# Attention front of a routed-expert kernel: values through four 32-row tiles, scores through two 64-row tiles

## The chip, the cores and the metric

The kernel runs on one core of one Trainium2 chip. The metric is the device time of one launch in microseconds, taken as the median of several runs. The engines named below are TensorE (PE for its matrix multiplications, PEld for its weight loads), VectorE (DVE), ScalarE (ACT), GpSimd (POOL) and SyncE (SP, which here only issues transfers).

## The reference

Two stages are computed. The first is an attention through 32 memory slots per head: for each of 8 batches and 8 heads, `phi` (576 tokens by 32 slots) is put through a softmax over the slots, keys and values are summed into the slots with these weights, and every query attends to the 32 slots. The second is a mixture of eight experts with exactly 576 tokens each: a greedy assignment by descending gate logit, then two matrix multiplications with a ReLU between them.

```python
a = exp(phi - max(phi)); a = a / (sum(a) + 1e-9)            # [8, 8, 576, 32]
k_m = einsum('bhsm,bhsd->bhmd', a, k); v_m = einsum('bhsm,bhsd->bhmd', a, v)
scores = (q @ k_m.T) / 8
attn = softmax(scores)                                       # over 32 slots
x = (attn @ v_m) as [4608 tokens, 512]
logits = x @ w_gate                                          # [4608, 8]
assigned = greedy by logit, 576 tokens to each expert
out[expert e] = relu(x[e] @ w1[e]) @ w2[e]                   # 512 -> 1024 -> 512
```

## The kernel before

**Front.** Function `front` computes the attention. The work of a batch is done once for each of the 8 batches: phi is loaded (`load_a`), its maximum is taken (`m1`, `mt`, `m2`, `bt`) and subtracted (`bs`, `sb`, on VectorE for the batches in `BD`, on GpSimd for the others), then the exponential (`ex`), the sums over tokens into the slots (`kv_`, 80 matrix passes in four column tiles, after `load_kv` has brought keys and values), the normalisers (`zm`, `zn`, `zs`), and the transposed keys (`kt`, `kb`) and values (`vc`, `vd`). `vg` and `vl` multiply the slot values by the gate weights and put the result in eight more columns beside the values, so that the router's logits come out of the same multiplication as the attention's output.

The queries come in 18 units of 256 tokens. Sixteen are half a batch each. Units 8 and 17 are the rests of four batches each; they use 32 tokens of each batch at a time, and are called rest units below. A unit goes through `SC` (scores; PSUM tile `sc`), `T1` (VectorE transposes 32 by 32), `MX` (maximum), `SB` (subtraction, GpSimd), `SE` (exponential, ScalarE), `SU` (sum and reciprocal, three VectorE instructions), `NM` (multiplication, GpSimd), `T2` (transposed back), `AV` (values, PSUM tile `av` out of three banks), `XC` (copy to `xs` on ScalarE), `ST` (store to the DRAM buffer `xd`). The head pairs of keys and values are kept as zero-padded operands: `kbd` holds each head's 64 rows of keys with 64 rows of zeros, and `vb` holds four heads' values as blocks of a 128 by 256 matrix whose other blocks are zeros, cleared once at the start (L1063).

For 13 units the logits come out of `AV`, in columns 256 to 263 of each of its four outputs, and VectorE copies or adds them into `lg` (`LO`, L1021 and L1024). For the five units in `DF` an own multiplication `LG` gives the logits early (`LC` copies them, L1017), and `AV` may come later.

All of these operations are ordered by a planner (`build`, `Sched`): it is given each operation's engine, a duration, what it needs, and a key, and writes one fixed program order for each engine. The engines then run their own lists in order and wait for each other by semaphores. The table `PRMS` holds the keys.

**Router.** From the logits, `r1` (four groups of token columns) finds each token's best margin, `sg` to `tT` find a threshold for every expert, `assign` picks the experts, `p1`, `p4a` and the `ll` multiplications make lists of token rows (`idx`). With the first five columns of `idx`, GpSimd gathers token rows from `xd` (L415).

**Experts.** `FFN.run` then works off eight experts. Each expert's weights are loaded, split in two parts of lower precision, and three multiplications are added for each product. This stage isn't touched.

The lines of the kernel that the prediction uses: L907 and L910 are `kv_`, L914 and L915 `zm`, L970 `SC`, L1006 `AV`, L1014 `LG`, L853 the load of keys and values, L856 that of a unit's queries, L1038 and L1043 the stores.

Of the kernel before, what the change touches and what calls it, by code (L numbers as in the profile page):

```python
# [67 lines left out]
class Router:  # L68
# [6 lines left out]
    def __init__(s,tc,lg,cf,fo,cb,bo,keep,out=None,ident=None):  # L75
# [9 lines left out]
        s.kp=keep; s.pq={}; s.lists={}; s.keep_il={}  # L85
    def begin(s,wk,ps,small,T,pos,il):

        s.wk=wk; s.ps=ps; s.small=lambda sh: ps.tile(sh,F32,name=small,bufs=2)
        s.tg=(pos,il)
        s.T=ps.tile([128,E],F32,name=T[0],bufs=T[1])  # L90
# [90 lines left out]
    def p1(s):  # L181
        nc=s.nc
        s.pos=s.ps.tile([128,289],F32,name=s.tg[0][0],bufs=s.tg[0][1])
# [39 lines left out]
    def RT(s,a,i):  # L223
        R,Rt,*x=s.lists[a]
        s.nc.vector.tensor_tensor(Rt[:,i],R,x[i],op=ALU.mult)
        if i and s.keep_il.get(a) is None:
            s.lists[a][4]=s.ps.tile([128,2,R.shape[2]],F32,name=s.tg[1][0],bufs=s.tg[1][1])
            if a: s.keep_il[a]=s.lists[a][4]
        if i: s.lists[a][4]=s.keep_il.get(a,s.lists[a][4])
# [386 lines left out]
class Sched:  # L616
# [67 lines left out]
    P=8.03, TQ=-25.59, CQ=-371.99, SC=-17.05, T1=-43.99, MX=38.12, SB=167.02, SE=6.14, T2=-53.03,  # L684
    AV=172.87, AVS=0.46, SU=-19.2, NM=22.34, XC=-91.14, LO=-48.45, ST=-63.73, EV=15, NP=3, NB=7, NQ=9,
    NK=2,
    UB=[4.67, 3.41, -1.23, -0.5, -5.71, -9.21, -5.08, 5.12, 2.83, -10.67, -26.24, 4.6, -0.08, 22.96, 4.55, 2.18, 2.71, 0.03],
    CF=163.65, CB=176.37, NA=3, BD=[0, 1, 2, 7], DF=[12, 13, 14, 15, 16], LG=56.71, LC=208.16,
    DA=305.18, DX=292.62, DS=238.38, R0=159.09, RK=-963.03, W1=257.31, WH=177.42, WS=304.44, WE=0,
    RV=[26, 10], la=-39.88, lk=-23.18, lq=3.93, lr=-16.74, m1=132.78, mt=-2.4, m2=-95.66, bt=3.2,  # L690
    bs=32.51, sb=5.74, ex=-99.2, ad=71.74, kv=-50.81, kvs=-2.43, zm=-31.99, zn=28.86, zs=88.73,
    vc=17.65, kt=30.28, vd=-43.5, kb=-149.94, vg=-8.21, vl=18.54,
    PB=[16.49, -24.8, 8.73, 2.34, -0.04, 30.67, -11.48, 4.98], slack=0, wend=30,
)
def build(X,f,B=8):
# [9 lines left out]
    for n in range(N):  # L705
        T=anch[n]+X['UB'][n]; b,bb,_=units[n]; rem=len(bb)>1
        op('SP',(1.35,3.3),T+X['SC']+X['lq'],lambda n=n:f.load_q(n),[],[('lq',n)],[('Q',X['NQ'],('Q',n))])
        for h in range(2):
            op('PE',1.1 if rem else .6,T+X['SC']+.5*h,lambda n=n,h=h:f.SC(n,h),[('lq',n)]+[('kb',x) for x in bb]+([('sc',n,0)] if h else []),[('sc',n,h)],[] if h else [('sc',1,('sc',n))],[('Q',n),('sc',n)]+[('KB',x) for x in bb])
# [9 lines left out]
        if df:  # L719
            op('PE',.9,T+X['LG'],lambda n=n:f.LG(n),[('t2',n)]+[('vl',x) for x in bb],[('lgm',n)],[('tp',2,('lgm',n))],[('pT',n)]+[('VB',x) for x in bb])  # L720
            op('DVE',.16,T+X['LC'],lambda n=n:f.LC(n),[('lgm',n)],[('lg',n)],[],[('lgm',n)])
        ta,tx,ts=(X['DA']+n,X['DX']+n,X['DS']+n) if df else (T+X['AV'],T+X['XC'],T+X['ST'])
        for j in range(4):
            op('PE',.56 if rem else .45,ta+X['AVS']*j,lambda n=n,j=j:f.AV(n,j),[('t2',n)]+[(i,x) for x in bb for i in ('vc','vl')],[('av',n,j)],[('av',X['NA'],('av',n,j))],[('pT',n)]+[('VB',x) for x in bb])
            if not df: op('DVE',.15,T+X['LO']+X['AVS']*j,lambda n=n,j=j:f.LO(n,j),[('av',n,j)]+([('lo',n,j-1)] if j%2 else []),[('lo',n,j)],[],[('av',n,j)])
            act=1 if df else X['EV']>>j&1
            op('ACT' if act else 'DVE',.32 if act else .4,tx+X['AVS']*j,lambda n=n,j=j,e=act:f.XC(n,j,e),[('av',n,j)]+([('xc',n,0)] if j else []),[('xc',n,j)],[] if j else [('x',3,('x',n))],[('av',n,j),('x',n)])
# [409 lines left out]
```

## Time and profile before

| | |
|---|---|
| Median of 3 runs | 575.54 us (571.08 to 579.89) |
| Profiled execution | 571.48 us, of which its span is 569.7 us |
| PE, DVE, ACT, POOL busy, share of the span | 93%, 78%, 52%, 49% |
| Mean granted TensorE clock | 0.976 |
| Front to the last group of logits | 0 to 141 us |
| Router to the first five index columns | 141 to 156 us |
| Gathering, rest of the indices | 156 to 164 us |
| Experts | 164 to 570 us |

Busy time counts an engine's instructions. For PE the ends of matrix passes are modelled, so that a pass seems to last some 0.27 us although the next one starts much earlier; the time that a row of many passes takes is therefore read from the span of the whole row. An fp32 multiplication of the code is two records in the profile, each a weight load and a pass.

### The profile page before, as it was taken

To read this page: it belongs to the slowest core of one execution; us is meant where nothing else is said; L and a number is where in the kernel's file an instruction comes from. 1 tells how busy PE (TensorE), PEld (TensorE's weight loads), DVE (VectorE), ACT (ScalarE), POOL (GpSimd) and SP (SyncE) were. 2 spreads that over 40 slices of the span, in tenths; PEclk is the share of its full clock that TensorE was granted. 3 is DMA by queue.
4 is the path that set the end of the run, shared out by engine and by line. 5 is a ranking of instruction groups with operands and counts; after the bars stand their busy time and mean duration, and the time that the engine had idled before them with its cause. 6 is when DMAs were issued, how large, how long until landed. Compare 5 with 4: busy or idle time off the path is not lost.

```text
span 569.7 us, 11439 instructions
## 1 busy us (share of the span) xinstructions
PE 530.6 (93%) x4336; PEld 449.8 (79%) x4336; DVE 446.8 (78%) x820; ACT 293.8 (52%) x633; POOL 278.4 (49%) x251
## 2 busy tenths in 40 slices
PE   7997989978769999999999999999999999999993
PEld 2675766766359988988997998899899889889982
DVE  3378898796824499999999789989989988999500
ACT  2245556464415464773685466467466636746310
POOL 6277876475060095457438426733742851472011
PEclk9999899998959999999999999999999999999998
DMA  8999999932264737744952872693487178223010
GB/s 302 417 413 414 367 355 363 327 155 96 92 192 121 230 118 228 247 138 144 291 173 73 292 216 71 190 318 103 118 279 231 37 223 287 84 104 127 1 47 37
DMA packets 52592, 114.23 MB, mean 201 GB/s; under 512 B 6512, under 2 KB 23920, under 8 KB 50480
## 3 DMA queue, kind: packets, MB, share of 16 engines
q1 hardware_dynamic: 44128, 85.36, 45.0%
q0 software_dynamic: 5904, 19.14, 9.8%
q10 hardware_dynamic: 2496, 8.91, 3.9%
q8 instruction: 36, 0.59, 0.4%
q14 instruction: 28, 0.23, 0.1%
HBM read 86.13 MB, written 27.26 MB: 199 GB/s over the span
## 4 chain that ended last, share of the span: by engine, by line
PE 46%; issue 12%; POOL 5%; DVE 5%; DMA 2%; ACT 1%; another core or an unknown queue 1%; POOLq 0%; ACTq 0%; DVEq 0%
PE ph L465 22%; PE py L483 18%; PE py L472 3%; POOL out L488 3%; PE ph L453 2%; DVE w1l L392 2%; POOL st L384 1%; DMA out<-y,idx 1%; DVE hl L456 1%; DVE xr L445 1%; PE ph L435 1%; DMA st<-in_moe_w 1%; DVE cc L467 1%; POOL g L422 0%
## 5 line engine op out<-in xcount | busy, mean ns | idle before, releaser
L483 PE MATMUL py<-w2h,hl 128*128 128x512 f32 x256 | 100.4, 392 | 0.4 <-DVE hl L456 0.4
L483 PE MATMUL py<-w2h,hh 128*128 128x512 f32 x256 | 100.4, 392 | 0.0
L483 PE MATMUL py<-w2l,hh 128*128 128x512 f32 x256 | 100.3, 392 | 0.0
L488 POOL DMA_INDIRECT out<-y,idx x32 | 49.5, 1547 | 59.6 <-ACT y L485 55.3
L483 PEld LDWEIGHTS py<-w2h,hl 128*128 128x128 f32 x256 | 48.1, 188 | 11.0 <-DVE hl L456 0.8
L483 PEld LDWEIGHTS py<-w2l,hh 128*128 128x128 f32 x256 | 48.1, 188 | 10.7
L483 PEld LDWEIGHTS py<-w2h,hh 128*128 128x128 f32 x256 | 48.1, 188 | 10.5
L384 POOL TENSOR_TENSOR s<-st 128x512 f32<-128x512 f32 x14 | 18.9, 1349 | 75.9 <-DMA st<-in_moe_w 47.9
L456 DVE SCALAR_TENSOR_TENSOR hl<-cc,hh 128x288 fp32r<-128x288 f32 x84 | 50.7, 624 | 2.2 <-ACT hh L455 2.1
L465 PE MATMUL ph<-xh,w1h 128*128 128x288 f32 x224 | 48.2, 296 | 1.7 <-ACT p L548 0.9
L465 PE MATMUL ph<-xh,w1l 128*128 128x288 f32 x224 | 47.9, 294 | 0.0
L465 PE MATMUL ph<-xl,w1h 128*128 128x288 f32 x224 | 47.9, 295 | 0.0
L422 POOL DMA_INDIRECT g<-xd,idx x28 | 33.1, 1183 | 28.2 <-DMA xp<-g 21.6
L384 POOL TENSOR_TENSOR st<-st 128x512 f32<-128x512 f32 x28 | 45.0, 1610 | 1.3
L455 ACT ACTIVATE hh<-cc 128x288 fp32r<-128x288 f32 x84 | 35.2, 442 | 11.7 <-DVE cc L467 8.2
L407 DVE TENSOR_TENSOR w2l<-st,w2h 128x1024 fp32r<-128x1024 f32 x32 | 40.0, 1253 | 1.0 <-ACT w2h L406 0.6
L1029 ACT COPY xs<-av 128x256 f32<-128x256 f32 x72 | 25.4, 373 | 28.9 <-PE av L1006 24.5
L384 POOL TENSOR_TENSOR st<-s,st 128x512 f32<-128x512 f32 x14 | 22.9, 1638 | 35.5 <-DVE w1l L392 15.6
L392 DVE TENSOR_TENSOR w1l<-st,w1h 128x1024 fp32r<-128x1024 f32 (+1 forms) x28 | 39.6, 1432 | 0.5 <-ACT w1h L391 0.5
L465 PEld LDWEIGHTS ph<-xh,w1h 128*128 128x128 f32 x224 | 36.2, 188 | 3.0 <-DVE v L467 1.3
L485 ACT COPY y<-py 128x512 f32<-128x512 f32 x32 | 18.7, 583 | 35.4 <-PE py L483 33.5
L391 ACT CAST s1h<-st 128x512 fp32r<-128x512 f32 x42 | 25.9, 618 | 21.2 <-POOL st L384 21.2
(191 smaller groups left out, 1345.6 us busy)
## 6 DMA issues: line engine op xcount, KB each, us to landing
st<-in_moe_w SPq DMA_DIRECT2D x64, 512.0 KB
kv<-in_k SPq DMA_DIRECT2D x8, 1152.0 KB
kv<-in_v SPq DMA_DIRECT2D x8, 1152.0 KB
qm<-in_q SPq DMA_DIRECT2D x18, 512.0 KB
xd<-xs ACTq DMA_DIRECT2D x16, 512.0 KB
xp<-g SPq DMA_DIRECT2D x112, 64.0 KB
ts<-xp SPq DMA_DIRECT2D x28, 256.0 KB
pt<-in_phi SPq DMA_DIRECT2D x8, 576.0 KB
```

The source lines that it names most:

```text
L384: s.nc.gpsimd.tensor_tensor(o,x,y,op=ALU.subtract if i else ALU.add)
L391: def whi(s,e,c,i): h,l,x=s.wop(e,c,i); s.nc.scalar.copy(h,x)
L392: def wlo(s,e,c,i): h,l,x=s.wop(e,c,i); s.nc.vector.tensor_tensor(l,x,h,op=ALU.subtract)
L407: def l2c(s,j): (s.nc.gpsimd if j in WP else s.nc.vector).tensor_tensor(s.w2l[j],s.R2[j],s.w2h[j],op=ALU.subtract)
L422: s.nc.gpsimd.indirect_dma_start(out=g,out_offset=None,in_=xd,in_offset=bass.IndirectOffsetOnAxis(ap=idx[:,c:c+1],axis=0))
L455: def rh(s,f,j,c): s.nc.scalar.activation(s.hh[:,f,j],c[:,:288],AF.Relu)
L456: def rl(s,f,j,c): s.nc.vector.scalar_tensor_tensor(s.hl[:,f,j],c[:,:288],0.0,s.hh[:,f,j],op0=ALU.max,op1=ALU.subtract)
L465: s.nc.tensor.matmul(c[:,:288],s.W(w,a)[:,k,m],x[:,b,k],start=start and n==0,stop=n==5,skip_group_check=not start); n+=1
L483: nc.tensor.matmul(py,a[:,f,j,o],b,start=(f==0 and q==0),stop=(f==7 and q==2))
L485: def full_y(s,c,py): s.Y[c]=y=s.yp.tile([128,D],F32,name="y"); s.nc.scalar.copy(y,py)
L488: s.nc.gpsimd.indirect_dma_start(out=out.pop(),out_offset=bass.IndirectOffsetOnAxis(ap=ix,axis=0),in_=s.Y.pop(c)[:n],in_offset=None)
L1029: (nc.scalar.copy if act else nc.vector.tensor_copy)(U[n,'x'][:,u,256*hh:256*hh+256],U[n,'av',j][:,:256])
```

## The change

Values: `vb` keeps 128 rows (four heads of 32 slots) by 64 values and 8 logit columns, without zero blocks. `AV` takes for each head of a group the 32 rows of that head, as its own row tile of the array, and the four row tiles of a group write to four PSUM banks. Scores: `kb` keeps 128 rows (two heads of 64) without zeros, and `SC` takes 64 rows at a time, two row tiles that write to two banks. The logits of all 18 units come from `LG`; `LO` is gone. `XC` is two copies of 512 columns in place of four of 256, each reading four banks. PSUM is fixed: two banks for scores (`SCT`), four for values (`AVT`), two for the rest; the router's tiles lie in these banks, so that `p1` waits for the last `XC`. All stores of `xs` are issued from SP. There are nine `xs` buffers in place of three and seven query buffers in place of nine. `BD` gains batch 3, `DF` is [8, 11, 13, 16, 17] in place of [12, 13, 14, 15, 16], and all keys of `PRMS` are new. The zeroing of `kbd` and `vb` is gone, `vc` is one copy in place of four, `kb` one in place of two.

```diff
-    AV=172.87, AVS=0.46, SU=-19.2, NM=22.34, XC=-91.14, LO=-48.45, ST=-63.73, EV=15, NP=3, NB=7, NQ=9,
+    SU=11.0, NM=-19.59, XC=-59.99, ST=33.7, NP=3, NB=7, NQ=7, NK=2, XB=9,
...
         def vc(b):
-            for i in range(4):
-                r=slice(32*i,32*i+32)
-                nc.gpsimd.tensor_copy(vb[r,:,64*i:64*i+64],kvn[r,:,1,0,:])
+            nc.gpsimd.tensor_copy(VB[vs[b]][:,:,:D],P[b,'kvn'][:,:,1,0,:])
...
         def SC(n,hh):
-            for u in range(2):
-                for m,bb in enumerate(bs):
-                    for i in range(4):
-                        nc.tensor.matmul(sc[32*i:32*i+32,u,hh,w*m:w*m+w],KBD[ks[bb]][:,4*hh+i,u,:],qT[:,4*hh+i,w*m:w*m+w],start=True,stop=True)
+            for m,bb in enumerate(bs):
+                for i in range(4):
+                    for u in range(2):
+                        nc.tensor.matmul(sc[32*i:32*i+32,u,128*hh+w*m:128*hh+w*m+w],KB[ks[bb]][64*u:64*u+64,4*hh+i],qT[64*u:64*u+64,4*hh+i,w*m:w*m+w],start=True,stop=True)
...
-        def AV(n,j):
-            u,hh=j//2,j%2
+        def AV(n,u):
...
-            U[n,'av',j]=av=ps.tile([128,C],F32,name="av",bufs=PRMS["NA"])
-            for m,bb in enumerate(bs):
-                nc.tensor.matmul(av[w*m:w*m+w],pT[:,u,hh,w*m:w*m+w],VB[vs[bb]][:,hh,:C],start=True,stop=True)
+            for hh in range(2):
+                for m,bb in enumerate(bs):
+                    for i in range(4):
+                        r=slice(32*i,32*i+32)
+                        nc.tensor.matmul(AVT[w*m:w*m+w,i,U[n,'av'],128*u+64*hh:128*u+64*hh+64],pT[r,u,hh,w*m:w*m+w],VB[vs[bb]][r,hh,:D],start=True,stop=True)
...
+            nc.scalar.copy(U[n,'x'][:,u].rearrange("p (h i d) -> p i h d",h=2,i=4),AVT[:,:,U[n,'av'],128*u:128*u+128].rearrange("p i (h d) -> p i h d",h=2))
...
-                    nc.scalar.dma_start(xo[b*S:b*S+512].rearrange("(p c) d -> p c d",c=4)[:,2*u:2*u+2],xs)
+                    nc.sync.dma_start(xo[b*S:b*S+512].rearrange("(p c) d -> p c d",c=4)[:,2*u:2*u+2],xs)
...
-    A('PE',.35,'p1',[('assign',)])
+    A('PE',.35,'p1',[('assign',)]+[('xc',n,j) for n in range(N) for j in range(2)])
```

The change moves operations in every engine's list. Three places follow.

SP's list before, at the loads for the last batches (`kv` a half of keys or values, `qm` a unit's queries, `pt` phi):

```order
L853 DMA kv_158<-in_k 128x2304
L856 DMA qm<-in_q 128x1024
L850 DMA pt_154<-in_phi 128x1152
L853 DMA kv_158<-in_v 128x2304
L850 DMA pt_155<-in_phi 128x1152
L853 DMA kv_157<-in_k 128x2304
L856 DMA qm<-in_q 128x1024
L853 DMA kv_157<-in_v 128x2304
```

and the same place of SP's list after the change:

```order
L843 DMA pt_157<-in_phi 128x1152
L1018 DMA xd<-xs 128x1024
L846 DMA kv_159<-in_k 128x2304
L849 DMA qm<-in_q 128x1024 x2
L846 DMA kv_159<-in_v 128x2304
L1018 DMA xd<-xs 128x1024 x3
L846 DMA kv_160<-in_k 128x2304
L849 DMA qm<-in_q 128x1024 x2
L846 DMA kv_160<-in_v 128x2304
```

Stores (`xd<-xs`) of finished units now stand between the loads; the last three before the load of the last batch's keys (`kv_160`) are those of units 7, 6 and 9.

PE's list before, from the normalisers of the last batch (L914, L915; the `kvn` row transposes its keys):

```order
L915 MATMUL tp<-ones,al_126 128x1
L949 MATMUL tp<-wgs,vbd_124 64x8 x4
L1006 MATMUL av<-vb_131,pT 128x264
L970 MATMUL sc<-qm,kbd_122 32x128 x16
L1006 MATMUL av<-vb_131,pT 128x264
L935 MATMUL tp<-id,kvn 128x128 x4
L1014 MATMUL tp<-vb_132,pTd 128x8 x4
L970 MATMUL sc<-qm,kbd_121 32x128 x8
```

and after:

```order
L908 MATMUL tp<-ones,al_126 128x1
L955 MATMUL sc<-qm,kb_122 32x128 x16
L1001 MATMUL tp<-vb_132,pT 128x8 x4
L992 MATMUL av<-vb_132,pT 128x64 x16
L926 MATMUL tp<-id,kvn 128x128 x4
L955 MATMUL sc<-qm,kb_116 32x128 x16
L992 MATMUL av<-vb_132,pTd 128x64 x8
```

Before, the scores of units 12, 13, 15, 16 and 17 stood behind the last batch's sums; after, those of 11, 15, 16 and 17 do, and half the values of a unit are eight multiplications of 64 columns where they were two of 264.

PE's list after the change in the router (L135 gives the thresholds' steps, L149 the counts, L163 the broadcast thresholds). Before, only clock-keeping multiplications stood between these rows:

```order
L945 MATMUL sc<-wb 128x512
L135 MATMUL tp<-rc,cf 96x4
L992 MATMUL av<-vb_131,pTd 32x64 x4
L992 MATMUL av<-vb_133,pTd 32x64 x4
L992 MATMUL av<-vb_132,pTd 32x64 x4
```

and further down, where the first of two rows is the last of the rest unit's values:

```order
L992 MATMUL av<-vb_127,pTd 32x64 x4
L163 MATMUL sc<-id,Te 128x8
```

The values of unit 17, a rest unit, are now multiplied inside the router, 32 multiplications between L135 and L149 and 32 between L149 and L163.

More of the change, by code (lines that the diff above doesn't have):

```diff
@@ L182, in p1 @@
         nc=s.nc
-        s.pos=s.ps.tile([128,289],F32,name=s.tg[0][0],bufs=s.tg[0][1])
+        s.pos=s.banks[0][:,:289]
         nc.tensor.matmul(s.pos,s.b('tri'),s.ohz,start=True,stop=False)
@@ L225, in RT @@
         s.nc.vector.tensor_tensor(Rt[:,i],R,x[i],op=ALU.mult)
[L226 to L229, printed above, removed]
+        if i: n=R.shape[2]; s.lists[a][4]=s.banks[1+(a>0)][:,:2*n].rearrange("p (i n) -> p i n",i=2)
     def ll(s,a,ts):
@@ L758, in build @@
     GR=Router.GR
-    lgs=lambda g:[t for n in range(N) for u in (0,1) if GR[g][0]<=units[n][2]+u<GR[g][1] for t in ([('lg',n)] if n in X['DF'] else [('lo',n,2*u+1)])]
+    lgs=lambda g:[t for n in range(N) for u in (0,1) if GR[g][0]<=units[n][2]+u<GR[g][1] for t in [('lg',n)]]
     for g in range(4):
@@ L824, in front @@
         NB=PRMS['NB']; vs={}; ks={}
-        KBD=[cp.tile([128,8,2,M],F32,name=f"kbd{i}") for i in range(NB)]
+        KB=[cp.tile([128,8,M],F32,name=f"kb{i}") for i in range(NB)]
         VBD=[cp.tile([128,2,4,M],F32,name=f"vbd{i}") for i in range(2)]
         AL=[cp.tile([128,2,4,M],F32,name=f"al{i}") for i in range(2)]
-        VB=[cp.tile([128,2,264],F32,name=f"vb{i}") for i in range(NB)]
+        VB=[cp.tile([128,2,D+8],F32,name=f"vb{i}") for i in range(NB)]
         wb=W.wb=keep.tile([128,256],BF,name="wb"); nc.vector.memset(wb,0.0)
```

111 lines of the change are left out of this document (46 added, 65 removed).

## The prediction

> **What bounds the kernel now.** I read the stages first, from the busy times by window, then the row of the DMA engines on the page.
>
> ```profile
> 28.00:105.00 77.00, 69.44 (x1270) 51.97 (x1268) 62.26 (x160) 40.55 (x99) 55.41 (x67) 0.98 0.99 378
> 105.00:141.00 36.00, 29.98 (x406) 22.88 (x407) 29.98 (x79) 18.78 (x44) 23.98 (x21) 0.91 0.45 175
> 164.00:570.00 406.00, 393.90 (x2291) 354.40 (x2290) 329.84 (x518) 221.22 (x459) 180.57 (x128) 0.99 0.52 163
> DMA  8999999932264737744952872693487178223010
> ```
>
> Columns: stretch and its length, then busy time of PE, weight loads, DVE, ACT, POOL, the granted clock, the DMA share and GB/s. The experts' stage is full of PE work (393.9 of 406 us); the change does not reach it, it only starts earlier or later. In the front no engine is full alone. From 28 to 105 us PE has 69.4 of 77 us and DVE 62.3; from 105 to 141 us both have 29.98 of 36. The transfers are saturated up to about 110 us, but 378 GB/s are only needed as far as an engine waits for data, and the waits name other engines:
>
> ```profile
> PEld av L1006 <- DVE lg L1021: 2.2, 7, 0.6
> PEld av L1006 <- issue: 2.0, 9, 0.3
> PEld sc L970 <- DVE lg L1021: 1.6, 2, 1.4
> PEld av L1006 <- DVE lg L1024: 1.3, 3, 0.7
> PEld av L1006 <- ACT xs L1029: 1.1, 3, 0.7
> SPq L853 <- PE tp L910: 19.9, 5, 8.3
> ```
>
> Total, number, longest. PE waits for the logit copies and value copies that free the three `av` banks; the loads of keys and values wait for PE to free their two buffers. So the front is bound by PE and DVE in turn, each with some idle time caused by the other. What the change is worth is therefore worked out once for each of the two engines, and I take a value between.
>
> **DVE's sum.** The logits first:
>
> ```profile
> L1024 DVE TENSOR_TENSOR lg<-av,lg 128x8 f32<-128x8 f32 x26 | 4.2, 160 | 1.3 <-ACT xs L1029 0.5 <-PE av L1006 0.4
> L1021 DVE COPY lg<-av 128x8 f32<-128x8 f32 x26 | 4.2, 160 | 4.1 <-ACT xs L1029 3.9
> L1017 DVE COPY lg<-tp 128x16 f32<-128x16 f32 x5 | 0.9, 183 | 0.7 <-PE tp L1014 0.6
> ```
>
> 52 copies and additions go, 8.4 us; 13 more copies of the kind L1017 come, 13 x 0.183 = 2.4. That is -6.0. The idle time in front of them goes too (4.1 + 1.3 = 5.4); the new copies wait 0.7/5 each, 13 x 0.14 = 1.8, so -3.6. Then the stores, which leave ACT's queue. One place shows their price:
>
> ```profile
> 101.41 2.88 ACTq L1043 DMA_DIRECT2D xd<-xs  x4
> 104.33 0.63 ACT L984 ACTIVATE p<-p 128x512 f32<-128x512 f32 x1 [2.79 <-issue]
> 104.99 0.69 DVE L988 TENSOR_REDUCE z<-p 128x16 f32<-128x512 f32 x1 [2.44 <-ACT p L984]
> ```
>
> Four stores hold ACT for 2.8 us, the exponential behind them is late, and DVE stands for 2.44 us: -2.4. Batch 3's subtraction moves from GpSimd to DVE, but its place is before 28 us, where DVE waits for phi and PE: 0, and at most its own length:
>
> ```profile
> L877 DVE TENSOR_TENSOR pt<-pt,tp 128x1024 f32<-128x1024 f32 x4 | 4.8, 1211 | 2.2 <-PE tp L875 2.2
> ```
>
> (1.2 us). DVE's sum is -6.0 - 3.6 - 2.4 = **-12.0 us**.
>
> **PE's sum.** Pass lengths come from rows of many passes.
>
> ```profile
> 87.04 2.09 PE L1006 MATMUL av<-vb,pT 128*128 128x264 f32 x8
> 108.69 0.97 PEld L1014 LDWEIGHTS tp<-vb,pTd 128*128 128x128 f32 x8
> 66.42 0.81 PEld L970 LDWEIGHTS sc<-qm,kbd 128*32 128x32 f32 x32 [0.34 <-issue]
> 121.77 1.19 PEld L970 LDWEIGHTS sc<-qm,kbd 128*32 128x32 f32 x128 [0.33 <-DVE rv L100]
> ```
>
> A unit's values take 2.09 us in 8 passes now and will be 32 passes, each loading 128 columns for 32 rows and streaming 64. No row tile is in the trace, so I bound a pass. Below stands the cheapest row, 128 passes of four column tiles in 1.19 us, 0.009 each: 0.3 us a unit. Above stands the load of 128 columns with next to nothing to stream, 0.97/8 = 0.12, if four row tiles don't overlap: 3.9 us. I take overlap by four, as the column tiles show: a quarter of 0.12, plus half of the 0.025 that 128 streamed columns cost in the 66.42 row, is 0.043, or 1.4 us a unit. That saves 0.7 in 16 units, -11.2. The two rest units get 128 short passes; 1.2 us at 0.009, 3.2 at 0.025, against 2.0 now: 0, bounds -1.6 and +2.4 for both.
>
> The Trainium skill, TensorE: Matmul & The Clock Gate, gives 3.07 times for four row tiles of 32 rows at 512 columns (Part 3). No run here shows it; as an estimate, 32 passes of 0.12 + 0.05 us over 3.07 would be 1.8 us a unit, and PE's sum 6 us higher.
>
> `LG` comes to 13 more units at 0.97 each: +12.6. It stands in the path of the logits of the last units, where `AV` stood before. Scores go from four to eight tiles at once; bounds 0.81 (nothing gained) and 0.4 a unit, I take 0.6: 18 x -0.2 = -3.8. A change of the array's layout shows as a gap of 2.0/9 = 0.22 us (the "issue" row above); values now have a layout of their own, one more change a unit, +4.0. Work: -11.2 + 12.6 - 3.8 + 4.0 = +1.6. The waits for logit and value copies listed above go: 2.2 + 1.6 + 1.3 + 1.1 = -6.2. A new wait comes: with four banks one unit's `AV` must wait for both copies of the unit before. In PE's list that is back to back for units 11 and 15 only, with the scores of no unit but the logits of 16 and 17 behind it; two copies of 128x512 from PSUM cost as the experts' do,
>
> ```profile
> L485 ACT COPY y<-py 128x512 f32<-128x512 f32 x32 | 18.7, 583 | 35.4 <-PE py L483 33.5
> L1029 ACT COPY xs<-av 128x256 f32<-128x256 f32 x72 | 25.4, 373 | 28.9 <-PE av L1006 24.5
> L930 POOL COPY vb<-kvn 32x128 f32<-32x128 f32 x32 | 9.9, 311 | 9.2 <-ACT kvn L925 8.2
> ```
>
> 1.2 us and the semaphores: +1.4, bounds 0 (copies done) and 3. PE's sum is 1.6 - 6.2 + 1.4 = **-3.2 us**, with bounds of about -26 (value passes at 0.009, the other low ends) and +45 (0.12, the high ends).
>
> ACT gets 36 copies at 583 ns, 21.0, for 25.4 us; GpSimd's `vc` shrinks from four copies to one, and the zeroing goes. ACT (40.6 of 77) and GpSimd (55.4 of 77) are no bound, and GpSimd's zeroing lies beside the first loads: 0. If either were the bound it would be a gain.
>
> **Between the two.** Neither engine decides everywhere: the middle of -12.0 and -3.2 is -7.6.
>
> **Router.** The values of unit 17, 128 passes, now lie in it. What is there now:
>
> ```profile
> 142.16 0.30 PE L136 MATMUL tp<-rc,cf 16*96 16x4 f32 x2 [0.24 <-ACT xs L1029]
> 143.51 0.16 PE L150 MATMUL tp<-cn,cb 96*96 96x2 f16 x1 [0.27 <-DVE ok L121]
> 144.43 0.22 PE L164 MATMUL sc<-id,Te 8*128 8x8 f32 x1
> 146.86 0.30 PE L184 MATMUL qp<-oh,cb 128*128 128x289 f16 x1 [0.38 <-DVE oh L179]
> 156.16 1.41 POOL L415 DMA_INDIRECT st<-xd,idx  x1 [18.14 <-DVE idx L237]
> ```
>
> The first half (0.6 to 1.6 us) has 1.05 us before the counts, the second 0.76 before the thresholds; both have a layout change. I take +0.7, bounds 0 and +2.5. `p1` (L184) also waits for both copies of unit 17, 1.2 us after the second half; the mask between L164 and L184 takes 2.4, and covers it. Behind `p1` the SP store of unit 17 is issued 9 us before the gather at 156.16. The sum is -7.6 + 0.7 = **-6.9 us**.
>
> The profiled execution took 571.48 us (span 569.7), so it would give 564.6; the median shown is 4.1 higher, 575.54, and from there the forecast is 568.6, rounded to **569**.
>
> **Rivals.**
>
> *Row tiles one after another (slower).* Each row tile's load of 128 columns costs its full 0.12 us. That is 2.5 us more for 16 units than I took, +40 for PE. The Trainium skill, TensorE: Matmul & The Clock Gate (LDWEIGHTS), states that a load costs by its columns and not its rows, which speaks against cutting a unit's values into four times as many loads; the trace has no load of 32 rows. PE's idle time from 28 to 141 us is 113 - 99.4 = 13.6 us, which swallows that much: 575.5 - 3.2 + 40 - 13.6 + 0.7 = 599. It decides from 13.6/512 = 0.027 us above my 0.043 a pass on, about 0.07. For it: no row shows row tiles. Against it: column tiles overlap well below one load's length. 0.15.
>
> *Loads late behind stores (no change).* SP now holds a load back until a store's copies are done. The last batch decides:
>
> ```profile
> 77.42 0.33 SPq L853 DMA_DIRECT2D kv<-in_k  x1
> 101.29 1.08 PE L907 MATMUL tp<-kv,at 128*32 128x128 f32 x32 [0.26 <-issue]
> ```
>
> Its keys are asked for when PE has freed the buffer, and used 24 us later. After the change the store of unit 9 stands ahead: its logits, values and copies end about 6 us after that moment; two halves of 1.2 MB and two units of 0.5 MB at 378 GB/s are 9 us more. 15 of 24 us: it fits, with 7 to 9 us left. If the copies slip more, every microsecond counts; 8 us give 577. 0.13.
>
> *The whole front loosens (faster).* DVE idles 20.8 us from 28 to 141 us, of which I removed 6.0. In the new order two units' scores stand ahead of the last batch's sums, so less is left for DVE behind them; if the sums come no later, the work of one and a half units leaves the tail, where a unit costs
>
> ```profile
> L975 DVE STREAM_TRANSPOSE p<-sc 128x512 f32<-128x512 f32 x18 | 12.6, 700 | 1.3 <-PE sc L970 1.3
> L978 DVE TENSOR_REDUCE mx<-p 128x16 f32<-128x512 f32 x18 | 12.2, 675 | 0.1
> L988 DVE TENSOR_REDUCE z<-p 128x16 f32<-128x512 f32 x18 | 12.1, 672 | 5.3 <-ACT p L984 5.0
> L989 DVE TENSOR_SCALAR z<-z 128x16 f32<-128x16 f32 x18 | 8.2, 457 | 0.6
> L990 DVE RECIPROCAL z<-z 128x16 f32<-128x16 f32 x18 | 4.6, 253 | 0.6
> L998 DVE STREAM_TRANSPOSE pT<-p 128x512 f32<-128x512 f32 x13 | 8.9, 683 | 0.5 <-POOL p L993 0.5
> ```
>
> together 3.4 us: -12.0 - 5.1 + 0.7 = -16.4, or 559. Against it: PE has the extra `LG` ahead of these sums (11 units, 10.7 us). 0.22.
>
> **How the numbers follow.** Forecast 0.50, tiles in turn 0.15, loads late 0.13, looser front 0.22. A run of this kernel tells about 2% from no change: 564.0 and 587.1. Faster gets the looser front and 0.05 of the forecast, 0.27; slower the tiles in turn and 0.02 for a mixture with late loads, 0.17; the same 0.56. The range reaches from a little below 559 to where the tile rival is half true, 590, and leaves out its full 599: 556 to 590.
>
> **What would show it.** Right: rows of 32 value passes spanning about 1.4 us; one copy per unit of the logits; no idle time of DVE behind value copies; the router 0.7 us longer between its first multiplication and its thresholds; the first gather at about 149 us (156.16 before). Wrong: value rows of 3 to 4 us; PE waiting for `kv`; the normalisers of the last batch much later than 105 us; SP waiting long for ACT with loads behind it.

## Result and profile after

The changed kernel took 594.05 us (median of 4 runs, 590.51 to 597.21); the kernel before took 573.9 us in the same session. The ratio is 1.037 (95% interval 1.027 to 1.047): slower, where 569 us was forecast with a range of 556 to 590. Some executions of a kernel are over 1.5% slower than its fastest, at a lower clock; the ratios in this document leave these slow runs out, the medians do not.

The profiled execution took 597.21 us. First its stages, in the columns of the prediction (stretch, length, busy time of PE, weight loads, DVE, ACT, POOL, granted clock, DMA share, GB/s):

```profile
28.00:105.00 77.00, 71.94 (x1258) 61.35 (x1259) 50.81 (x114) 28.37 (x57) 39.14 (x39) 0.66 0.79 293
105.00:141.00 36.00, 29.72 (x641) 24.52 (x640) 18.17 (x43) 11.76 (x24) 12.82 (x14) 0.74 0.77 266
46.00:64.00 18.00, 17.68 (x237) 15.00 (x237) 10.61 (x26) 7.58 (x15) 9.20 (x8) 0.50 0.71 252
190.00:595.30 405.30, 393.78 (x2291) 354.26 (x2291) 327.68 (x521) 221.03 (x459) 178.46 (x128) 0.98 0.51 163
```

The experts (last row) do the same 2291 passes in 405.3 us that they did before in 405.7 (from 164 us to the end of the span). The loss is all ahead of them, and there one column stands out: the granted clock is 0.66 from 28 to 105 us, where it was 0.98. In that stretch PE and its weight loads are busier than before, the other engines less. Note the third row: PE has 17.68 of 18 us and still gets half its clock. The page shows it along the whole span, in 40 slices of 14.9 us of the kernel after, and below of 14.2 us of the kernel before:

```profile
PEclk9985756775566999999999999999999999999997
```

```profile
PEclk9999899998959999999999999999999999999998
```

What half a clock does is seen in PE's timeline after, in the same three steps of a unit at clock 1.00 and later at 0.50 (start, length of the row, and the count at its end):

```profile
113.13 1.06 PE L1001 MATMUL tp<-vb,pT 128*128 128x8 f32 x8
114.12 1.12 PE L992 MATMUL av<-vb,pT 32*128 32x64 f32 x32
116.16 0.67 PE L955 MATMUL sc<-qm,kb 64*32 64x128 f32 x32
...
129.95 1.10 PE L955 MATMUL sc<-qm,kb 64*32 64x128 f32 x32
130.98 1.87 PE L1001 MATMUL tp<-vb,pT 128*128 128x8 f32 x8
132.78 1.99 PE L992 MATMUL av<-vb,pT 32*128 32x64 f32 x32
```

and a unit's scores before, at clock 1.00:

```profile
66.42 1.08 PE L970 MATMUL sc<-qm,kbd 128*32 128x128 f32 x32
```

The row tiles do what they are made for: a unit's values take 1.12 us for 2.09 before, its scores 0.67 for 1.08. At half clock nearly all of it is given back. And the unchanged work pays too, as the groups of PE's instructions between 28 us and the first gather show, after and then before (count, busy time, mean ns of one, idle time ahead):

```profile
L992 PE MATMUL av<-vb,pT 32*128 32x64 f32 x416 | 24.1, 394 | 2.4 <-ACT xs L1009 2.4
L1001 PE MATMUL tp<-vb,pT 128*128 128x8 f32 x104 | 20.9, 329 | 0.1
L900 PE MATMUL tp<-kv,at 128*32 128x128 f32 x384 | 18.8, 354 | 5.9 <-issue 4.3 <-DMA kv<-in_v 1.2 <-ACT p L969 0.3
```

```profile
L907 PE MATMUL tp<-kv,at 128*32 128x128 f32 x384 | 13.2, 274 | 0.7 <-issue 0.5 <-DVE vb L952 0.2
```

The same 384 passes of `kv_` take 18.8 us for 13.2. At clock 1.00 the first two groups would be 13 x 1.12 = 14.6 and 13 x 1.06 = 13.8 us, so the clock costs 9.5 + 7.1 + 5.6 = 22 us in these three groups alone (an estimate: it puts all that exceeds the time at clock 1.00 down to the clock). The first gather comes at 182.93 us for 156.16:

```profile
182.93 1.50 POOL L411 DMA_INDIRECT st<-xd,idx  x1 [20.57 <-DVE idx L233]
```

One of the falls of the clock comes behind a wait. PE stands for 4.32 us in the middle of the last batch's sums, for a reason that the profile doesn't name; up to 127.5 us the clock is 1.00, behind that it is 0.50, and it stays there until 175 us:

```profile
127.29 0.31 PE L900 MATMUL tp<-kv,at 128*32 128x128 f32 x4 [4.32 <-issue]
```

```profile
128.00:175.00 47.00, 42.03 (x673) 33.67 (x670) 29.44 (x74) 16.63 (x31) 17.89 (x13) 0.50 0.39 141
```

The falls at 45.5 and at 72.9 us come in full rows of PE, without a wait.

There is a second finding, on SP's queue, whose waits after the change from 20 to 135 us are (total, number, longest):

```profile
SPq L1018 <- ACT xs L1009: 59.6, 10, 12.6
SPq L846 <- PE tp L903: 15.6, 3, 6.9
```

```profile
87.53 16.67 SPq L1018 DMA_DIRECT2D xd<-xs  x3
104.30 0.38 SPq L846 DMA_DIRECT2D kv<-in_k  x1
```

SP stands 59.6 us with stores that wait for copies, loads behind them. Three stores hold it from 87.53 to 104.2 us, and the last batch's keys are asked for only then, at 104.30 us (77.42 before). So there were two suspects: what the matrix engine is given to do costs it its clock, or the loads come late, PE waits, and the clock falls for that.

### The profile page after: what moved, and what is told of

The parts are those of the page before. It is cut to its first block, busy times and chain, and to the rows that moved or that the text cites. A ratio compares the mean times of both kernels' runs of the same rounds, so it can differ in the third digit from the quotient of the medians.

```text
span 595.3 us, 12768 instructions
## 1 busy us (share of the span) xinstructions
PE 555.8 (93%) x5060; PEld 481.4 (81%) x5060; DVE 442.1 (74%) x783; ACT 285.6 (48%) x588; POOL 259.5 (44%) x211
## 4 chain that ended last, share of the span: by engine, by line
PE 71%; issue 10%; DVE 7%; DMA 5%; POOL 2%; ACT 1%; SPq 1%; POOLq 0%; DVEq 0%; ACTq 0%
PE py L479 21%; PE ph L461 19%; PE av L992 5%; PE ph L449 4%; PE tp L1001 4%; PE py L468 4%; PE tp L900 4%; PE sc L955 2%; POOL out L484 2%; PE sc L945 2%; DMA kv<-in_v 2%; DVE w1l L388 1%; DMA st<-xd,idx 1%; DVE hl L452 1%; DMA ts<-xp 1%
## 5 line engine op out<-in xcount | busy, mean ns | idle before, releaser
L452 DVE SCALAR_TENSOR_TENSOR hl<-cc,hh 128x288 fp32r<-128x288 f32 x84 | 48.8, 602 | 2.5 <-ACT hh L451 2.3
L418 POOL DMA_INDIRECT g<-xd,idx x28 | 31.9, 1138 | 33.0 <-DMA xp<-g 27.2
L1009 ACT COPY xs<-av 128x512 f32<-128x512 f32 x36 | 20.3, 587 | 35.5 <-PE av L992 32.2
L461 PEld LDWEIGHTS ph<-xl,w1h 128*128 128x128 f32 x224 | 36.0, 187 | 0.0
```

Of the source, the lines that this page charges most:

```text
L418: s.nc.gpsimd.indirect_dma_start(out=g,out_offset=None,in_=xd,in_offset=bass.IndirectOffsetOnAxis(ap=idx[:,c:c+1],axis=0))
L452: def rl(s,f,j,c): s.nc.vector.scalar_tensor_tensor(s.hl[:,f,j],c[:,:288],0.0,s.hh[:,f,j],op0=ALU.max,op1=ALU.subtract)
L461: s.nc.tensor.matmul(c[:,:288],s.W(w,a)[:,k,m],x[:,b,k],start=start and n==0,stop=n==5,skip_group_check=not start); n+=1
```

## Experiments

Ratios are to the kernel before, run again in the same session, with their 95% intervals; clocks are those from 28 to 105 us of one profiled run, if nothing else is said. The edits are shown abridged, the probes' and the planner's as a summary.

**What brings the clock down: the forms alone.** Stretches of one kind, without waits, ahead of the kernel's own work.

```diff
+for g,n in ((pAV,320),(pSC,480),(pLG,80),(pFV,40),(pFS,320),(pTR,128),(pUN,8)):
+    dense(60); g(n)
```

> Ahead of the changed kernel's own work TensorE runs seven stretches on the loaded queries, one after another and back to back: the value tiles of 32 rows (320 instructions), the score tiles of 64 rows (480), the 8-column logit products (80), values as 128 rows by 256 columns (40), scores as 128 rows by 32 columns (320), transposes (128), and eight times what a unit issues (scores, logits, values). Ahead of each stand 60 dense bf16 products of 128x512, so that each begins at the granted clock 1.00. The kernel's total time means nothing here. Theory (the clock follows how much of the array works, not how long TensorE is busy): with TensorE busy throughout, the clock falls to 0.50 within some 10 us in the logit products at least, probably in the value tiles of 32 rows or the unit mix, and stays 1.00 in the 128-row values. Rival (the clock falls because TensorE waits in the front): all seven stretches stay at 1.00, since nothing waits here. Rival (the row tiles run one after another): at clock 1.00 a value instruction takes over 0.13 us; the trace of the changed kernel has 1.12 us for 16, 0.07 us each.

Windows of the probe; in this order the value tiles, score tiles, 8-column logit products, 128-row values, 128-row scores, transposes, and the unit mix without its first 4 us:

```profile
16.00:34.00 18.00, 18.00 (x641) 17.91 (x642) 0.00 (x0) 0.00 (x0) 0.00 (x0) 1.00 0.02 5
47.00:71.00 24.00, 15.16 (x961) 13.32 (x962) 0.00 (x0) 0.00 (x0) 0.00 (x0) 1.00 0.02 4
84.00:116.00 32.00, 32.00 (x161) 31.72 (x161) 0.00 (x0) 0.00 (x0) 0.00 (x0) 0.53 0.00 1
131.00:148.00 17.00, 17.00 (x80) 14.93 (x80) 0.00 (x0) 0.00 (x0) 0.00 (x0) 1.00 0.00 0
161.00:179.00 18.00, 18.00 (x643) 17.55 (x643) 0.00 (x0) 0.00 (x0) 0.00 (x0) 1.00 0.01 4
192.00:206.00 14.00, 14.00 (x129) 13.86 (x128) 0.00 (x0) 0.00 (x0) 0.00 (x0) 1.00 0.00 1
223.00:253.00 30.00, 30.00 (x461) 26.82 (x461) 0.00 (x0) 0.00 (x0) 0.00 (x0) 0.50 0.01 2
```

The 8-column products fall to half clock while PE is busy without a gap (the ends of its passes are modelled, but the weight loads alone are busy for 31.72 of 32 us); the score tiles hold 1.00 although PE pauses for 9 of 24 us, 1.1 to 1.7 us at a time. Value tiles hold it too, which I had put among those that probably fall. The mix of the three falls: no wait is needed. A value instruction takes 18.0/320 = 0.056 us, so the tiles do run beside each other.

The Trainium skill, TensorE: Matmul & The Clock Gate (HAM oscillation), states as a rule that PE must have no idle gaps of over some 3.4 us. By that rule the third and the last row would be at full clock and the second is no danger; the second agrees, as does the fall behind the wait of 4.32 us, but the third and the last do not. In these rows a full PE does not hold the clock by itself; what its products put through the array seems to matter too, which the third probe tests.

**How the mixes stand.**

```diff
+for mix in ([SC,AV],[SC,LG72,AV],[SC,AV72],[SC128,LG,AV],[SC,LG,AV128],[SC128,AV128]):
+    dense(60); 8 units of mix
```

> Ahead of the changed kernel's own work six mixes of eight units each run back to back, each behind 60 dense bf16 products of 128x512: (1) scores in 64-row tiles, values in 32-row tiles; (2) the same with logit products of 72 columns between; (3) scores in 64-row tiles, values of 72 columns in 32-row tiles, no logit products; (4) scores of 128 rows, 8-column logit products, values in 32-row tiles; (5) scores in 64-row tiles, 8-column logit products, values of 128 rows by 256 columns; (6) scores and values of 128 rows, no logit products. The total time means nothing. In the first probe the 8-column logit products alone fell to 0.50 within 10 us, value tiles and score tiles alone stayed at 1.00, and the mix of all three fell within 4 us. Theory (the separate 8-column logit products bring the mix below what holds the clock): 1, 3 and 6 stay at 1.00, 4 falls, 2 stays at 1.00 and takes no longer per logit product than 0.27 us, 5 falls late or not at all. Rival (going from tile form to tile form costs the clock): 1, 2 and 3 fall as well, and only 6 stays.

Windows of the six mixes, in that order:

```profile
16.00:29.00 13.00, 13.00 (x508) 10.95 (x496) 0.00 (x0) 0.00 (x0) 0.00 (x0) 1.00 0.02 5
42.00:64.00 22.00, 22.00 (x579) 18.91 (x578) 0.00 (x0) 0.00 (x0) 0.00 (x0) 1.00 0.01 3
77.00:91.00 14.00, 13.73 (x513) 11.32 (x503) 0.00 (x0) 0.00 (x0) 0.00 (x0) 1.00 0.01 4
104.00:128.00 24.00, 24.00 (x572) 21.78 (x568) 0.00 (x0) 0.00 (x0) 0.00 (x0) 1.00 0.01 3
141.00:168.00 27.00, 27.00 (x384) 21.59 (x383) 0.00 (x0) 0.00 (x0) 0.00 (x0) 1.00 0.01 2
182.00:205.00 23.00, 23.00 (x313) 17.72 (x306) 0.00 (x0) 0.00 (x0) 0.00 (x0) 1.00 0.01 1
```

All six hold. Only the changed kernel's own mix falls: back to back, all three parts of it are needed, and taking any one back is enough (4 was expected to fall and does not). In the mix that falls the 8-column products are 0.99 of 2.64 us, in mix 4 0.99 of 3.05. By that share the edge lies between. Mix 2 is the same instructions with 72 columns, at 2.69 us a unit for 2.64: holding the clock costs next to nothing there.

**How many columns hold it.**

```diff
+for w in (16,24,32,40,48,64,80): dense(60); 80 logit products of w columns
```

> Ahead of the changed kernel's own work seven stretches of 80 logit products each, back to back, with 16, 24, 32, 40, 48, 64 and 80 columns, each behind 60 dense bf16 products of 128x512. The total time means nothing. With 8 columns such a stretch fell to clock 0.50 after some 5 us. Theory (the clock counts the columns that run through the array, not the time TensorE is busy): the stretches with few columns fall to 0.50 and take 0.4 us an instruction, those with many hold 1.00 at 0.26 us, with one border between; from the mix of the three products, which falls with 0.99 us of 8-column products in 2.64 us and holds with 0.99 in 3.05 us, the border would be at some 40% of the columns that fit into an instruction, 20 to 30. Rival (weights loaded for every instruction bring the clock down, whatever the columns): all seven fall.

PE's timeline of the probe, the stretches of 48 and 64 columns:

```profile
195.74 28.67 PE L1074 MATMUL av<-kv 128*128 128x48 f32 x160
...
239.59 17.97 PE L1074 MATMUL av<-kv 128*128 128x64 f32 x160
```

A border, as expected, but at 48 to 64 columns and not at 20 to 30. More columns are faster here: 18.0 us for 64 of them, 28.7 for 48. 80 columns take 18.0 us as well, and the narrow stretches run at the same rate until their clock falls: some 0.22 us for each product of the code, which is two of the passes counted here.

**One part of the change taken back, or its cost taken away.** Five kernels, each an edit of the changed one.

```diff
+for k in range(8): nc.tensor.matmul(AVT[:,k%4,buf],wb[:,:128],wb[:,:256])     # e1, ahead of AV
-... pT[r,u,hh], VB[r,hh,:64] ...  +... pT[:,u,hh], VB[:,hh,:256] ...            # e2
-... KB[64*u:64*u+64], qT[64*u:64*u+64] ...  +... KB[:,4*hh+i,u], qT ...          # e3
-nc.sync.dma_start(xo[...],xs)  +nc.scalar.dma_start(xo[...],xs)                 # e4
-matmul(lm,pT,VB[:,hh,64:])  +matmul(lm,pT,VB[:,hh,:])                           # e5
```

> The changed kernel with eight bf16 products of 128x256 on zeros ahead of each unit's values, into the banks that the values then overwrite. Eight are 0.9 us at clock 1.00 and 1.8 us at 0.50, 16 to 32 us for the 18 units. Theory (clock follows the work in the array): the granted clock between 28 and 105 us rises from 0.66 to above 0.8, and the front gets no longer or gets shorter in spite of the added work: first gather between 160 and 182 us (182.93 before), total 572 to 594. Rival (the clock falls because of waits, or is not what made the front longer): the clock stays near 0.66 and the added work shows in full, total 605 to 625.

> The changed kernel with the values alone taken back to zero-padded operands of 128 rows (128x256 products into the same four banks, copies and order of the program as in the changed kernel; GpSimd places the values in four copies again). Theory, if the value tiles carry the loss of clock: the granted clock between 28 and 105 us is above 0.9, a unit's values take about 2.1 us as in the kernel before, first gather at 156 to 166 us, total 568 to 578. If the score tiles or the logit products carry it, or the new order of stores and work: the clock stays below 0.8, a unit's values take over 3 us and the total is 600 or more.

> The changed kernel with the scores alone taken back to a zero-padded key operand of 128 rows (ScalarE places the keys in two copies again). If the score tiles carry the loss of clock: granted clock between 28 and 105 us above 0.9, total 568 to 580. If the value tiles or the logit products do: clock up by less than 0.1, total 588 to 600, since a unit's scores go from 0.67 to 1.08 us at clock 1.00 in exchange for a little more work in the array.

> The changed kernel with all stores of its values issued from ScalarE's queue again, at the places of the order where SyncE issues them now. Theory (clock by the mix on TensorE): granted clock between 28 and 105 us within 0.05 of 0.66, total 588 to 602. Rival (loads wait behind stores on SyncE's queue, TensorE waits, the clock falls for that): the clock above 0.8 and a total of 565 to 582.

> The changed kernel with 72 columns instead of 8 through each logit product (the values' 64 columns go along and are not read). Same number of instructions, same order, no other edit. Theory (the 8-column products bring the array's work below what holds the clock): a logit product takes no longer than the 0.27 us it takes at clock 1.00 now, since its 128 columns of weights have to be loaded anyway; the granted clock between 28 and 105 us rises from 0.66 to above 0.85, and the total falls to 565 to 582. Rival (the tile forms or the waits cost the clock): clock within 0.05 of 0.66, total 590 to 605.

The windows from 28 to 105 us, e1 to e5 (one kernel a fence):

```profile
28.00:105.00 77.00, 68.39 (x1344) 55.44 (x1350) 52.18 (x118) 29.28 (x60) 40.77 (x40) 0.85 0.81 301
```

```profile
28.00:105.00 77.00, 67.53 (x1169) 54.50 (x1168) 55.24 (x124) 31.23 (x64) 47.99 (x61) 0.93 0.85 315
```

```profile
28.00:105.00 77.00, 70.39 (x1270) 59.33 (x1268) 51.23 (x116) 30.78 (x63) 39.96 (x40) 0.79 0.79 294
```

```profile
28.00:105.00 77.00, 69.94 (x1343) 58.10 (x1344) 56.70 (x122) 31.43 (x64) 43.85 (x43) 0.76 0.96 366
```

```profile
28.00:105.00 77.00, 68.73 (x1456) 57.44 (x1458) 57.97 (x126) 31.92 (x65) 43.89 (x44) 0.84 0.91 341
```

| kernel | us | ratio |
|---|---|---|
| changed | 594.05 | 1.037 (1.027 to 1.047) |
| e1, added products | 596.08 | 1.038 (1.033 to 1.043) |
| e2, values of 128 rows | 579.74 | 1.010 (1.006 to 1.014) |
| e3, scores of 128 rows | 592.45 | 1.031 (1.025 to 1.037) |
| e4, stores from ScalarE | 589.76 | 1.030 (1.024 to 1.036) |
| e5, 72 logit columns | 590.91 | 1.032 (1.026 to 1.039) |

Each edit raised the clock, and e1 is the plainest. Its added products keep PE busy for 25.6 us up to the first gather (16 us at full clock), and the first gather comes at 182.56 us for 182.93:

```profile
L990 PE MATMUL av<-wb 128*128 128x256 bf16 x144 | 25.6, 336 | 5.7 <-issue 3.0 <-ACT xs L1012 2.7
```

The total lies 2 us above what the theory allowed, far from the rival's 605. e2 gives 14 of the 20 us back, though its values take nearly twice as long at full clock; it lies 2 us above its forecast. e3, e4 and e5 lie 2 to 4 us below the changed kernel, but their intervals overlap with its own, so that none of the three is shown to help alone. The totals of e4 and e5 lie in the ranges named for "the mix" and for "tile forms or waits", their clocks between the two theories of each. e4 brings the DMA share from 0.79 to 0.96 and the load of the last keys from 104.30 to 85.66 us, so the loads did wait behind stores; but neither the thin products alone nor the late loads alone make the 20 us. The median runs of e4 and e5 are 4 and 7 us above the profiled ones, so their clocks read a little high.

**Both repairs together.** Stores from ScalarE, 72 columns, and 32 columns of ones in the normalisers (`zm`); then with added products; then with values of 128 rows.

```diff
+matmul(kvp[:,i,128:160],...,ones)                 # e7, ones of 32 columns, with the edits of e4 and e5
+4 products of 128x256 ahead of AV                # e8 = e7 +
+values of 128 rows, as in e2                     # e9 = e7 +
```

> The changed kernel with both single repairs and a third of the same kind: 72 columns through each logit product, the stores issued by ScalarE, and the normalisers' products with 32 columns of ones instead of one. No instruction is added. The two repairs alone gave clocks of 0.84 and 0.76 between 28 and 105 us (0.66 in the changed kernel) and 591 and 590 us. Theory (two causes that feed one another: the mix on TensorE lies at the edge of what holds the clock, and waits for loads behind stores push it under): the clock above 0.9 and a total of 570 to 582, more than either alone. Rival (the clock is not what sets the front's length; its order of work is): clock above 0.85 but total 586 to 592.

> The kernel before in this list (wide logit products and normalisers, stores from ScalarE) with four bf16 products of 128x256 on zeros ahead of each unit's values: 0.45 us a unit at clock 1.00, 8 us in all if nothing hides them. Theory: the clock between 28 and 164 us comes to 0.95 or more, and the total to 566 to 578. Rival (TensorE's time, not its clock, is what lacks by then): 5 to 8 us above the kernel without them.

> The changed kernel with values as zero-padded products of 128 rows, stores from ScalarE, wide logit products and wide normalisers: of the change only the score tiles, the separate logit products and the new order are left. With the values alone taken back it was 579.7 us at a clock of 0.93. Theory: clock 0.97 or more up to 141 us; the loads no longer wait behind stores, so 566 to 576 us, the time of the kernel before within 1.5%. If the new order itself costs time beside clock and stores: 577 to 585.

e7: 582.26 us, 1.010 (1.006 to 1.014), clock 0.84 and behind 105 us 0.84 (0.74 in the changed kernel):

```profile
28.00:105.00 77.00, 66.83 (x1397) 54.69 (x1394) 56.72 (x124) 31.02 (x64) 43.29 (x42) 0.84 0.98 385
105.00:141.00 36.00, 29.26 (x811) 25.36 (x811) 28.66 (x63) 17.50 (x32) 21.92 (x19) 0.84 0.41 144
```

Two repairs that alone lie 3 and 4 us below the changed kernel lie 12 us below it together. That fits losses that feed one another, as expected, but it is not shown: e7 also has the wide normalisers, which no run tests alone on the changed kernel, and the single repairs are not clear of the noise. Not one instruction was added. e7 also shows how clock and time go together: in the eight runs that its ratio rests on the time goes from 576.78 us at a mean clock of 0.941 to 583.72 at 0.926, 4.6 us for each 0.01. e8, 590.75 us, 1.023 (1.014 to 1.032): the rival. Its 8 us of products come back as 8.5 us of time; the clock only went to 0.87. e9, 580.72 us, 1.010 (1.007 to 1.013), its first rows:

```profile
28.00:105.00 77.00, 66.22 (x1162) 52.88 (x1165) 55.61 (x124) 31.27 (x64) 46.62 (x57) 0.96 0.95 371
105.00:141.00 36.00, 32.22 (x601) 25.55 (x589) 28.48 (x64) 15.94 (x28) 21.98 (x26) 0.91 0.47 165
```

The clock is close to that of the kernel before (0.98 and 0.91), the loads are nearly as early (last keys at 85.45 us for 77.42), and still 1% is missing, where 566 to 576 us was expected. Clock and stores are not all.

**Parts of the change alone, on the kernel before.**

```diff
-AV: 264 columns, LO  +AV: 256 columns, LG (in an av bank) and LC for every unit    # b1
-nc.scalar.dma_start(xo[...],xs)  +nc.sync.dma_start(xo[...],xs)      # b2
+80 logit columns for the deferred units, 32 columns of ones          # b3
```

> The kernel before with one part of the change alone: every unit's logits by separate 8-column products ahead of its values (256 columns then instead of 264), one copy on VectorE instead of four; everything else as before. 13 units x 1.06 us are 13.8 us more of TensorE's time, VectorE is spared 52 copies of 0.16 us less 13 of 0.18, 6 us. Theory (the clock falls only where tile forms and 8-column products meet): the granted clock between 28 and 105 us stays above 0.95, and TensorE's added time shows in part: 576 to 588. Rival (8-column products bring the clock down in any company): clock under 0.85 and 590 or more.

> The kernel before with another part of the change alone: the stores of the values issued from SyncE's queue, at the places of the order where ScalarE issues them. Theory: loads wait behind stores that wait for copies, 28 to 105 us at a DMA share clearly under the 0.99 of before and a granted clock under 0.98, total 574 to 586. Rival (stores cost nothing on either queue): 571 to 576.

> The kernel before with the two edits alone that add columns and no instruction: 80 columns instead of 8 in the logit products of the five deferred units, 32 columns of ones instead of one in the normalisers. It stands at clock 0.98 between 28 and 105 us and 0.91 from 105 to 141 us. Theory: the clock behind 105 us rises a little, 568 to 574, at most 1% faster. If wider products cost time: 574 to 580.

b1: 582.11 us, 1.017 (1.008 to 1.026), clock 0.93:

```profile
28.00:105.00 77.00, 71.51 (x1226) 57.40 (x1225) 55.63 (x122) 37.33 (x89) 51.96 (x62) 0.93 0.92 350
```

The separate logit products in this form cost some 10 us. How that splits was not separated: PE has 13 x 1.06 = 13.8 us more to do, DVE stands 10.1 us ahead of the 13 new copies, and the mean clock of its runs is 0.965 for 0.971, which at e7's rate would be some 3 us (an estimate). It is large enough for the 1% left in e9, which has these products too; e7's clock is still under that of the kernel before, so its 1% need not be theirs. b2: 575.09, 1.006 (1.002 to 1.010): the stores alone cost 3 us. b3: 570.22, 0.994 (0.991 to 0.998), the only kernel here that is faster than both, if only by 0.6%; its clock behind 105 us was 0.81 in the profiled run, so the reason given in its expectation isn't shown.

**Without the separate products, and in other orders of work.**

```diff
-LG for 13 units  +AV with 72 columns a head, reduce_sum over the heads    # e6; e10 with the edits of e7 and products on zeros
-planner: SC .5, AV .6, LG .45  +SC .33, AV .56, LG 1.05, table fitted anew  # e11 on e7; e12 on e6 with the edits of e7
```

> The changed kernel without separate logit products for the 13 units whose values are not deferred: their 32-row value tiles take the 8 logit columns along (72 columns a head instead of 64), and VectorE adds up the eight heads' parts out of the banks, two sums a unit, in place of one copy. The planner puts the work in a new order by itself. Theory: 13 x 1.06 us of TensorE's time at clock 1.00 go, the mix without 8-column products holds the clock above 0.85 between 28 and 105 us, total 555 to 572, below the kernel before. Rival (the tile forms or the waits cost the clock): clock below 0.75, and the total 578 to 592, since less work runs at half clock.

> The changed kernel with the logit columns taken along in the value tiles of the 13 units that are not deferred, stores from ScalarE, wide logit products and normalisers for the rest, and eight bf16 products of 128x144 on zeros a unit ahead of the values (0.5 us). The merged form alone gave 584.2 us at a clock of 0.81, 0.59 behind 105 us. Theory: clock above 0.92 in both stretches and a total of 560 to 574, perhaps below the kernel before. Rival (its order of work makes it long): clock above 0.85, total above 580.

> The changed kernel with wide logit products and normalisers and stores from ScalarE (582.3 us so far), in another order of work: the planner is given the durations of the trace for scores (0.33 a half), values (0.56 a half) and logits (1.05, it counted 0.45), and its table of numbers is fitted anew to these. If the order drawn for too short logit products is what is left: 566 to 576. If it is not: 578 to 588.

> The form without separate logit products for the units that are not deferred (72 columns in the 32-row value tiles), wide logit products and normalisers for the rest, stores from ScalarE, and the planner's table fitted anew to the durations of the trace. 13 x 1.06 us of TensorE's time are gone against the changed kernel. If the clock holds (above 0.92 between 28 and 141 us): 556 to 570, below the kernel before. If TensorE then has so little to do that the clock falls below 0.85: 574 to 590.

e6: 584.16 us, 1.014 (1.007 to 1.022), clock 0.81 and behind 105 us 0.59, where 555 to 572 us was expected. e10: 603.89, 1.052 (1.045 to 1.059), clock 0.87 and behind 105 us 0.62. e11: 595.06, 1.040 (1.031 to 1.048), clock 0.80. e12: 599.58, 1.046 (1.038 to 1.054); its window:

```profile
28.00:105.00 77.00, 63.49 (x1292) 50.48 (x1281) 47.07 (x110) 27.03 (x55) 37.05 (x38) 0.71 0.89 339
```

In this window PE is busy for 8 us less than in the changed kernel, and the clock is hardly better. No fitted order helped; whether these lose by their order or by a matrix engine with too little to do was not separated, and the planner that drew them knows nothing of the clock.

## Why the prediction was wrong

**The step that failed is "PE's sum"**: it took every duration at the clock of the trace before, as if the clock were given. It came out at -3.2 us. The clock fell to 0.66 instead, and that alone added some 22 us to three groups of PE's rows. Term by term:

- Values, forecast 1.4 us a unit (-11.2 in all): 1.12 at full clock, 0.035 us a pass for my 0.043. The 3.07 times that the Trainium skill gives (TensorE: Matmul & The Clock Gate, Part 3) is for 512 columns. Here 8 passes of 128 rows and 72 columns take 1.04 us in mix 2, 0.13 each, against 0.035 for a pass of 32 rows and 64 columns: 3.7 times.
- Scores, forecast -0.2 a unit: -0.4. The 0.81 us that I started from was the row of the weight loads; PE's own row is 1.08 us.
- Layout changes, forecast 0.22 us each, +4.0 in all: about 0.12 each, some 2 us (an estimate from the rows at the end of this document).
- Logits, forecast +12.6: right as a size (13 x 1.06 = 13.8 at full clock), wrong in its meaning. It was booked as time; it was also 37% of a unit's PE time, in products of only 8 columns.
- The missing term: +22 us in three groups. That also explains the sign: the prediction had no case in which the same work takes PE longer.

**DVE's sum**, -12.0: the copies went as forecast (18 of 173 ns), but DVE waited 7.4 us ahead of them, where I took 1.8 for the new 13 and 0.7 for the other five, and it was no bound any more. With PE at half clock, taking the middle of two sums had no meaning. Taking the stores off ACT's queue was booked at -2.4; on SyncE they cost 3 (b2).

**Router**, forecast +0.7: from the last logits to the first gather it is 20.0 us (162.91 to 182.93) for 16.6 (139.56 to 156.16), +3.4, at a clock of 0.66 from 162 to 183 us. From the first multiplication to the thresholds it is 2.70 us for 2.27, the +0.4 in the place for which 0.7 was forecast; most of the rest stands behind the thresholds, where rows of 8 and 19 clock-keeping products last 3.57 and 5.29 us, for 1.90 and 3.84 with 8 and 17 before. **The wait of values for copies**, forecast +1.4: 2.4. **Experts**: untouched, as said.

**Rivals.** Row tiles one after another: false (the first probe). Loads late behind stores: true as a mechanism (59.6 us of SP's waits, last keys 27 us later, 19 of them gone in e4), too small alone: 4 us in e4, not clear of the noise, and 3 in b2. The looser front: false. Two of the signs named for "wrong" came: the last batch's normalisers, named at 105 us, ended at 130 us, and SP waited long for ACT. Value rows took 1.12 to 1.99 us, not 3 to 4, and PE's named waits for `kv` are only 1.2 us.

Shown: the three forms together bring the clock down without any wait; each repair raises it; taking the values back restores most of the clock (0.93) and 14 of the 20 us; clock and time go together in runs of one program; separate logits and the stores cost 10 and 3 us when added to the kernel before. Open: how the remaining 1% of e7 and e9 splits between clock, logits and order; whether the long fall behind 127 us comes from the mix or from the wait ahead of it; and why the fitted orders lose. No kernel here ran the value tiles at the clock of the kernel before, so what they would save there is not shown.

## What to carry to other kernels

Before pricing work on the matrix engine, ask what the change does to its clock: where other products get shorter, thin ones beside them take a larger share of its time, and an engine that is busy all the time can still be granted half. Where a product took no longer at 72 columns than at 8, as here within 0.05 us a unit, more columns are the first repair to try. Wider products alone and earlier loads alone were not clear of the noise here, and together with wider normalisers they were (12 us), so test repairs together too.

## What was not expected of the hardware

- Busy time alone does not set the clock: 32.00 of 32 us busy at 0.53 with 8-column products, 15.16 of 24 us busy at 1.00 with 64-row tiles.
- For fp32 products of 128 columns of weights the border is between 48 and 64 columns at some 0.22 us a product; 80 of them took 18.0 us with 64 columns and 28.7 with 48.
- A change between the layouts of row tiles takes time, but little. Value and score tiles in stretches of their own (first probe, 32 passes being 18.03/20 = 0.90 us and 2.02/4 = 0.51 us) and alternating (second probe), all at clock 1.00:

```profile
15.84 18.09 PE L1050 MATMUL av<-kv 32*128 32x64 f32 x640
51.51 2.02 PE L1054 MATMUL sc<-kv 64*32 64x128 f32 x128 [1.11 <-issue]
...
16.41 1.12 PE L1050 MATMUL av<-kv 32*128 32x64 f32 x32
17.46 0.67 PE L1054 MATMUL sc<-kv 64*32 64x128 f32 x32
18.06 1.12 PE L1050 MATMUL av<-kv 32*128 32x64 f32 x32
```

  A pair takes 18.06 - 16.41 = 1.65 us for 1.41, so that a change costs about 0.12 us (an estimate from these rows; what in the change takes it is not shown).
